# Decay attention in front of two MLPs: scores computed once, e normalised and transposed by TensorE, values' product in plain float32

## The chip, the cores and the metric

The kernel runs on one core of one Trainium2 chip. The metric is the device time of one execution in microseconds, the median of several runs. A profile of one execution gives, for each engine, every instruction with its start and its length. The engines are PE (TensorE), DVE (VectorE), ACT (ScalarE), POOL (GpSimd) and SP, whose queue issues most DMAs. The "granted clock" is the share of full speed at which TensorE was let run.

## The reference

Causal attention with a decay, over 4 batches of 8 heads with 576 positions of 64 numbers, feeds two MLPs over the 2304 tokens (512 to 2048 to 512 each).

```
scores = scale * np.matmul(q, k.transpose(0, 1, 3, 2))
cum    = np.cumsum(np.log(np.clip(f, 0.0001, 1.0)), axis=-1)
decay  = cum[:, :, :, None] - cum[:, :, None, :]
scores = np.where(causal, -1000000000.0, scores + decay)
scores = scores - np.max(scores, axis=-1, keepdims=True)
attn   = np.exp(scores)
attn   = attn / (np.sum(attn, axis=-1, keepdims=True) + 1e-09)
x      = np.matmul(attn, v)                       # heads side by side: 2304 x 512
h = x @ moe_w_in;  g = h * sigmoid(1.702 * h);  x2 = g @ moe_w_out
h = x2 @ moe2_w_in; g = max(h, 0) + alpha * min(h, 0); out = g @ moe2_w_out
```

## The kernel before

**Precision.** Where float32 accuracy is wanted, an operand is split into a rounded part in the type fp32r and the rest (hi and lo, by ACT L519 and by a subtraction, L524), and three fp32r products are added in PSUM: hi·hi, hi·lo, lo·hi. A plain float32 matmul does it in one instruction, more slowly.

**Units and chunks.** Attention goes by units of two heads of one batch, 16 in all, and a unit's queries in two chunks, 0 to 256 and 256 to 576 (CH). Batch 0, whose units come first chunk by chunk, uses the row-tiled path ("old" in the code): two heads at once, each in 64 rows of the array (L938, L1086), the operands transposed by TensorE (`load_pe`, L794). The other 12 units have stacked operands (`stack`; KA, KB, QA, QB), in which hi and lo parts and the rows for the decay share the 128 rows.

**What a chunk does.** `chunk` computes scores with queries in partitions, from the hi parts alone, to get each query's maximum: matmuls L925 to L938, a masked maximum by DVE (L952, with a second instruction that reads the accumulator), the two halves of the last 64 queries' row joined by POOL (L961). The maxima are turned into rows by TensorE (L969) and written, negated, into the query operand (L980 on ACT, L982 on DVE). `chunk2` then computes the scores again, all products, with keys in partitions (L1081, L1086); the subtraction of the maximum is part of the product. ACT takes the exponential (L1097, tile e); POOL zeroes the masked half of diagonal blocks (L998). `after_scores` splits e into eh (L519) and el (L524) and multiplies by the split values (L1044); narrow pieces and batch 0 use plain float32 instead (L1010 for the first chunk of batch 0, two heads each in 64 columns of the array; L1016). Columns of ones beside the values make the sums of e come out of the same matmuls. The result is normalised behind the product: in batch 0 and the last unit by transposes, a reciprocal and a multiplication on DVE (L1114 to L1130), elsewhere through copies u (L1136) and DMAs that spread the sums over partitions by way of a scratch in DRAM (`dscr`; L1139, L1144, L1146) with DVE's L1142, L1143 and L1150.

**Around it.** The normalised x lies in a ring `xr`. The first MLP's first product (L1180, 960 matmuls in blocks of 256, 320, 256, 320 and 384 tokens) runs as background work between the attention's matmuls. Behind attention come the rest of that product in another form (L1203), the second product (L1424), and the second MLP (L1203, L1606).

**What sets the order.** The class `Plan` collects all operations and schedules them once, when the program is built: by expected durations, priorities, tile pools and PSUM banks, a delay of 230 ns between engines (LAT), 105 ns for a change of tile mode on TensorE (SWITCH), and a holding-back of background work (TRIES). An operation may have several engines to choose from (`a_copy`, `a_out`, `a_sub`), where a bias by size (WC) holds DVE back for some. The result is a fixed program order on every engine, and every engine takes its own in order. Where the plan sees TensorE idle it puts in filler matmuls (L490). PSUM has eight banks, shared by pools with caps: ps_s (scores) 4, ps_m (maxima) 2, ps_v (value products) 3, ps_h (first MLP) 2, ps_x 2.

Of the kernel before, what the change touches and what calls it, by code (L numbers as in the profile page):

```python
# [16 lines left out]
BC = 0  # L17
WC = 1.2
# [7 lines left out]
SWITCH = 105.0  # L26
PADC = 8000.0
PAD0, PAD1, PADN, PADM = 1600.0, 130000.0, 220.0, 200.0
TRIES = [(60.0, 300.0, 400.0)]
# [56 lines left out]
class Plan:  # L86
# [37 lines left out]
    def plan(self, pen, hold_for, back):  # L124
# [27 lines left out]
        while avail:  # L152
# [95 lines left out]
def kernel(  # L248
# [51 lines left out]

    A0 = 100.0
# [12 lines left out]
    dscr = dram.tile([2 * BH, 2 * (S - SPLIT)], F32, name="dscr")  # L314
# [64 lines left out]
    p_v0 = sl("r", F32, [SPLIT // P, 2, P], (3, 0, NP))  # L379
    p_dq0 = sl("w", F32R, [1, SPLIT], (0, 8192, NP))  # L380
# [13 lines left out]
    p_z = sb("att", "Z", 2, [P, 2, P], F32R)  # L394
# [28 lines left out]
    ps_s = psum_pool(4)  # L423
    ps_m = psum_pool(2)
    ps_v = psum_pool(3)
# [61 lines left out]
    ident_r = const.tile([P, P], F32R, name="ident_r")  # L487
# [14 lines left out]
    b_id, b_idr, b_mask, b_mask2, b_cum, b_alpha = Buf(), Buf(), Buf(), Buf(), Buf(), Buf()  # L502
# [29 lines left out]
    def a_out(n):  # L532
        return [("ACT", c_act(n, True)), ("DVE", c_dve(n), BC + WC * n)]

# [42 lines left out]
    plan.add(a_copy(P), lambda e: copy(e, ident_r, ident), [b_id], [b_idr], -60)  # L577

    b_id2 = Buf()
    for i in range(2):  # L580
        plan.add(a_copy(64), lambda e, r=slice(64 * i, 64 * i + 64): copy(e, ident2[r], ident[r, r]), [b_id], [(b_id2, i)], -39)
    fill = {}

    def fills(rd, *sets):
        for nm, p, view, n, val, which in sets:
            for i in range(p.n)[which]:
# [4 lines left out]
                ], rd, [b], -40 if rd else -90 if nm == "mx" else -70)  # L591
# [1086 lines left out]
```

## Time and profile before

| | us |
|---|---|
| median of 3 runs | 978.47 (976.31 to 980.2) |
| the profiled execution, device time | 978.25 |
| its span in the profile | 976.5 |
| TensorE busy in the span | 958.9 (98%) |
| VectorE busy | 755.6 (77%) |
| ScalarE busy | 629.3 (64%) |
| GpSimd busy | 130.7 (13%) |

The span is what the profile covers, from the first instruction to the last; the device time holds 1.75 us more around it. Attention takes the first 342 us of the span, mixed with the first MLP's background work; up to 42 us batch 0 starts up. In the rows further down, "x48" counts instructions; in a timeline row a run of equal instructions on one line is one row, with the start of the first and the time to the end of the last. TensorE overlaps one instruction's end with the next one's start, so the time that an instruction takes from the engine is the distance from its start to the next start.

### The profile page before, as it was taken

Reading aid. Unit: us, or ns where it says so; the run is one execution under the profiler, and the core shown is the slowest. Engines: PE = TensorE matmul, PEld = TensorE weight load, DVE = VectorE, ACT = ScalarE, POOL = GpSimd, SP = SyncE. Lnnn points to the kernel's source line nnn. Section 1 sums busy time; section 2 is a strip of 40 time slices with the busy share of each in tenths; the row PEclk is TensorE's granted clock in tenths of the full one; section 3 lists DMA queues with packets and bytes.
Section 4 is the critical chain, followed back from the end, with each engine's and each line's share of the span. In section 5 each row is a group of like instructions: output and inputs, shape, how many; then the busy total and the mean of one; then the engine's idle time right before and its main releaser. Section 6 shows DMA issues by size and latency. Waiting matters only on the chain.

```text
span 976.5 us, 18451 instructions
## 1 busy us (share of the span) xinstructions
PE 958.9 (98%) x6343; PEld 899.6 (92%) x6343; DVE 755.6 (77%) x1635; ACT 629.3 (64%) x1310; POOL 130.7 (13%) x273
## 2 busy tenths in 40 slices
PE   8999999999999999999999999999999999999998
PEld 6788899899999999988888988999999999999998
DVE  4889977788877699946558785788668967887876
ACT  6778986888777558867667795575555743333332
POOL 4236643222222102100000000000000000000000
PEclk9999999999999999999999999999999999999999
DMA  7866634444443136757888685778738495543523
GB/s 140 183 196 182 161 88 119 95 98 93 110 106 75 54 104 226 214 176 256 285 324 277 219 254 188 245 267 297 281 114 308 163 381 197 155 148 109 152 76 99
DMA packets 190015, 176.16 MB, mean 180 GB/s; under 512 B 106480, under 2 KB 164736, under 8 KB 187616
## 3 DMA queue, kind: packets, MB, share of 16 engines
q1 hardware_dynamic: 189904, 174.96, 58.1%
q8 instruction: 50, 0.82, 0.4%
q14 instruction: 45, 0.37, 0.1%
q10 hardware_dynamic: 16, 0.01, 0.0%
HBM read 110.95 MB, written 63.90 MB: 179 GB/s over the span
## 4 chain that ended last, share of the span: by engine, by line
PE 82%; DVE 7%; ACT 4%; DMA 3%; issue 2%; SPq 1%; POOL 1%; DVEq 0%; ACTq 0%; POOLq 0%
PE bk L1203 23%; PE bk L1424 20%; PE bk L1606 19%; PE bk L1180 8%; PE bk L1081 3%; PE bk L1016 2%; PE bk L1044 2%; DVE bk L952 1%; DMA u<-dscr 1%; PE bk L1086 1%; DVE el L524 1%; ACT e L1097 1%; PE bk L927 1%; DMA wraw<-in_moe_w_in_dram 1%; DVE KB L524 1%
## 5 line engine op out<-in xcount | busy, mean ns | idle before, releaser
L1203 PE MATMUL bk<-x,wS 128*128 128x384 f32 x912 | 160.4, 335 | 0.3 <-DVE lx L1229 0.2
L1203 PEld LDWEIGHTS bk<-x,wS 128*128 128x128 f32 x912 | 158.1, 188 | 1.2 <-DVE lx L1229 0.5
L1180 PE MATMUL bk<-xh,w 128*128 128x320 f32 (+2 forms) x640 | 156.6, 309 | 0.0
L1424 PE MATMUL bk<-lh,w 128*128 128x512 f32 (+1 forms) x640 | 146.9, 369 | 0.0
L1424 PEld LDWEIGHTS bk<-lh,w 128*128 128x128 f32 x640 | 112.9, 189 | 19.8
L1180 PEld LDWEIGHTS bk<-xh,w 128*128 128x128 f32 x640 | 111.3, 189 | 2.0 <-issue 1.4
L1180 PE MATMUL bk<-xl,w 128*128 128x320 f32 (+2 forms) x320 | 97.3, 304 | 0.1
L952 DVE CUSTOM_DVE_ANT_0 bk<-bk,mask 128x288 f32<-128x288 f32 (+4 forms) x160 | 74.9, 497 | 19.9 <-PE bk L927 17.1
L524 DVE TENSOR_TENSOR ll<-lx,lh 128x512 fp32r<-128x512 f32 (+1 forms) x80 | 50.9, 637 | 49.2 <-PE bk L1424 34.4
L519 ACT CAST x<-x 128x768 fp32r<-128x768 f32 (+3 forms) x57 | 47.3, 858 | 61.6 <-PE bk L1606 47.5
L1424 PE MATMUL bk<-ll,w 128*128 128x512 f32 (+1 forms) x320 | 81.2, 368 | 0.0
L1097 ACT ACTIVATE e<-bk 128x320 f32<-128x320 f32 (+4 forms) x224 | 63.2, 363 | 19.3 <-PE bk L1081 8.3
L1606 PE MATMUL bk<-wS,x 128*128 128x256 f32 x567 | 70.5, 284 | 0.0
L1606 PEld LDWEIGHTS bk<-wS,x 128*128 128x128 f32 x567 | 69.1, 192 | 0.0
L524 DVE TENSOR_TENSOR x<-x,x 128x768 fp32r<-128x768 f32 (+3 forms) x59 | 57.0, 983 | 15.4 <-ACT x L519 15.0
L1606 PE MATMUL bk<-wS,lh 128*128 128x256 f32 x378 | 68.7, 284 | 0.0
L1424 PEld LDWEIGHTS bk<-ll,w 128*128 128x128 f32 x320 | 57.1, 189 | 9.7
L519 ACT CAST lh<-x 128x768 fp32r<-128x768 f32 (+3 forms) x38 | 31.4, 851 | 53.7 <-PE bk L1606 48.4
L1390 ACT ACTIVATE lx<-lx 128x512 f32<-128x512 f32 (+1 forms) x80 | 46.8, 587 | 29.6 <-DVE ll L524 27.0
L1180 PEld LDWEIGHTS bk<-xl,w 128*128 128x128 f32 x320 | 60.5, 189 | 0.8 <-DVE xl L524 0.3
L1606 PEld LDWEIGHTS bk<-wS,lh 128*128 128x128 f32 x378 | 59.0, 192 | 0.0
L519 ACT COPY lx<-bk 128x384 f32<-128x384 f32 x72 | 34.2, 479 | 33.2 <-PE bk L1203 18.0
(230 smaller groups left out, 2153.8 us busy)
## 6 DMA issues: line engine op xcount, KB each, us to landing
h2scr<-lx SPq DMA_DIRECT2D x96, 192.0 KB
wraw<-in_moe_w_in_dram SPq DMA_DIRECT2D x32, 512.0 KB
wraw<-in_moe_w_out_dram SPq DMA_DIRECT2D x32, 512.0 KB
lx<-h1scr SPq DMA_DIRECT2D x64, 256.0 KB
x<-h2scr SPq DMA_DIRECT2D x32, 512.0 KB
w2scr<-wS SPq DMA_DIRECT2D x5, 1792.0 KB
tscr<-wS SPq DMA_DIRECT2D x4, 1792.0 KB
wS<-tscr SPq DMA_DIRECT2D x4, 1792.0 KB
```

What stands on the lines that cost most here:

```text
L519: nc.scalar.copy(dst, src)
L524: E[e].tensor_tensor(dst, a, b, op=ALU.subtract)
L952: plan.add([("DVE", c_dve(c1 - c0))], lambda e, pm=pm, c0=c0, c1=c1, mk=mk, m0=m0, col=col, f0=f0: nc.vector.tensor_tensor_reduce(pm.ap[:, ...
L1016: nc.tensor.matmul(pb[hh].ap[:, c0:c1], vr.ap[:, t, hh, :], e32.ap[:, hh, e0:e0 + m], start=st, stop=sp, skip_group_check=True,)
L1044: nc.tensor.matmul(pb[hh].ap[:l.shape[1], s0 - q0:n], l, rhs.ap[:w, hh, :m], start=st, stop=sp, skip_group_check=True,)
L1081: nc.tensor.matmul(pss[hh].ap[:w, o_:o_ + m], x.ap[r, hh, a:a + w], y.ap[r, hh, s0 - q0:n], start=i == 0, stop=i == 1, skip_group_check=True)
L1097: plan.add([("ACT", c_act(x1 - x0, True))], lambda e, hh=hh, pss=pss, e32=e32, w=w, x0=x0, x1=x1: nc.scalar.activation(e32.ap[:w, hh, :x1 ...
L1180: nc.tensor.matmul(ph.ap[:, :n], w.ap[:, a, c, :], x[c // 2].ap[:, c % 2, :n], start=(c == 0 and j == 0), stop=(c == KT - 1 and j == 2))
L1203: nc.tensor.matmul(out.ap[:, :XH], wt(a, c), x.ap[:, b, c, :], start=(st and c == 0 and i == 0), stop=(c == 1 and i == 2), skip_group_chec ...
L1390: plan.add([("ACT", c_act(n))], lambda e: nc.scalar.activation(g.ap[:, :n], raw.ap[:, :n], AF.Gelu_apprx_sigmoid), [raw], [g], pri)
L1424: nc.tensor.matmul(py[d].ap[:, :n], w[:, a, d * P:(d + 1) * P], (lo if x else h).ap[:, :n], start=(k == 0 and (a, x) == (0, 0)), stop=(k = ...
L1606: nc.tensor.matmul(py[j].ap[:, t * HF:(t + 1) * HF], x.ap[:, q:q + P], w[:, o, a, :], start=(k == 0 and t == 0 and c == 0), stop=(k == NPA ...
```

## The change

Scores are computed once, with queries in partitions and all products (`chunk`: L915 row-tiled, L919 stacked, L908 for the last 64 queries through Z, which now holds hi and lo parts). DVE's masked reduction (L935) scales by −0.125 and takes the minimum, which stays as a column `ms` beside the queries. ACT's exponential (L944) uses that column as its bias and returns the row's sum into `ms`, over a tile ea, eb, ec or ed. DVE adds 1e-9 (L953; L949 adds the two halves of the last 64 queries too) and takes the reciprocal (L955), and e is scaled in place by it (`a_scale`: 84 times on POOL, L963, 60 times on ACT, L961). `chunk2` transposes e in blocks of 128×128 on TensorE (L994, 400 of them, plain float32), copies the blocks out of PSUM into eT (`a_out`, L512 on ACT 167 times, L514 on DVE 73 times), and multiplies values by eT in plain float32, two heads at once, each in 64 columns of the array (L1003). One copy takes the result to `xr`. The second pass of scores, the maxima's transposes and their negated copies, POOL's masks and L961, the splits of e and of the values, the copies u, the old normalisation and its 110 DMAs through `dscr` are gone. The identity in fp32r and the fills for ones columns are gone as well. Scores have 3 PSUM banks, transposes 3, value products 1; the tiles eb, ec, ed have one buffer each and eT three. The constants for the plan change too: WC from 1.2 to 0.6, a bias of its own for copies out of PSUM (WO_ = 0.3), 800 instead of 400 ns of holding back, 540 instead of 610 ns for issuing a DMA.

```
-WC = 1.2
+WC = 0.6
+WO_ = 0.3
-TRIES = [(60.0, 300.0, 400.0)]
+TRIES = [(60.0, 300.0, 800.0)]
-                free[QUEUE[eng]] = t + 610.0
+                free[QUEUE[eng]] = t + 540.0
...
-    ps_s = psum_pool(4)
-    ps_m = psum_pool(2)
-    ps_v = psum_pool(3)
+    ps_s = psum_pool(3)
+    ps_e = psum_pool(3)
+    ps_v = psum_pool(1)
...
     def a_out(n):
-        return [("ACT", c_act(n, True)), ("DVE", c_dve(n), BC + WC * n)]
+        return [("ACT", c_act(n, True)), ("DVE", c_dve(n), BC + WO_ * n)]
...
+    def a_scale(n):
+        return [("POOL", 280.0 + 0.8 * n, 0.0, True), ("ACT", c_act(n) + 30.0, 300.0), ("DVE", c_dve(n, True), 600.0, True)]
...
+                    for hh in range(2):
+                        for i, (x, y, r) in enumerate(((qb, kb, slice(0, P)), (qa, ka, slice(0, 66 if hh == 0 else P)))):
+                            nc.tensor.matmul(pms[hh].ap[:, f0:f0 + c1 - c0], x.ap[r, hh, a - q0:a - q0 + w], y.ap[r, hh, c0:c1], start=i == 0, stop=i == 1, skip_group_check=True)
...
-                        pm.ap[:, f0:f0 + c1 - c0], pm.ap[:, f0:f0 + c1 - c0], mk[:, m0:m0 + c1 - c0], 1.0, NEG,
-                        ALU.add, ALU.max, accum_out=mx.ap[:, col:col + 1],
+                        pm.ap[:, f0:f0 + c1 - c0], pm.ap[:, f0:f0 + c1 - c0], mk[:, m0:m0 + c1 - c0], -0.125, first(),
+                        ALU.add, ALU.min, accum_out=ms.ap[:, col:col + 1],
...
+                plan.add([("ACT", c_act(x1 - x0, True) + 30.0)], lambda e, pm=pm, t_=t_, i=i, x0=x0, x1=x1, f0=f0, mc=mc, sc=sc: nc.scalar.activation(
+                    view[t_, i](x0, x1), pm.ap[:, f0:f0 + x1 - x0], AF.Exp, scale=-1.0, bias=ms.ap[:, mc:mc + 1], accum_out=ms.ap[:, sc:sc + 1]
...
+                plan.add([("DVE", 70.0, 0.0, True)], lambda e, j=j: nc.vector.tensor_scalar_add(ms.ap[:, 6 + 2 * j:8 + 2 * j], ms.ap[:, 6 + 2 * j:8 + 2 * j], 1e-9), (), [(ms, ("s", 6 + 2 * j)), (ms, ("s", 7 + 2 * j))], pri)
...
+            plan.add([("DVE", 85.0)], lambda e, cs=cs: nc.vector.reciprocal(ms.ap[:, cs[0]:cs[-1] + 1], ms.ap[:, cs[0]:cs[-1] + 1]), (), [(ms, ("s", c)) for c in cs], pri)
...
+                        nc.tensor.transpose(pt.ap[:, i * P:(i + 1) * P], view[j, hh](t * P, t * P + P), ident)
...
+                for c0, c1, o in moves:
+                    plan.add(a_out(c1 - c0), lambda e, pt=pt, et=et, c0=c0, c1=c1, o=o: copy(e, et.ap[:, o:o + c1 - c0], pt.ap[:, c0:c1]), [pt], [(et, o)], pri)
...
+                    nc.tensor.matmul(
+                        pb.ap[64 * hh:64 * hh + 64, s0 - q0:n], vr.ap[:, t, hh], et.ap[:, hh * m:hh * m + m],
+                        start=t == 0, stop=t == nt - 1, skip_group_check=True, tile_position=(0, 64 * hh),
+                    )
...
+            plan.add(a_out(y - x), lambda e, x=x, y=y: copy(e, xr[:, hp, x % RING:x % RING + y - x], pb.ap[:, x - t0:y - t0]), [pb], keys, pri)
```

The plan is made anew, so the order changes on every engine. Three places:

On TensorE in the middle of attention, in the order before, the maxima's transposes, background matmuls and the second scores follow one another (bk is a PSUM bank, xh, xl and w are the first MLP's operands, MX the maxima):

```order
L969 MATMUL bk_92<-ident_r,MX_105 67x128 x2
L969 MATMUL bk_92<-ident_86,MX_105 67x64
L1180 MATMUL bk_89<-xh_1012,w_1036 128x256
L1180 MATMUL bk_89<-xl_650,w_1036 128x256
L1180 MATMUL bk_89<-xh_1012,w_1036 128x256 x2
L1180 MATMUL bk_89<-xl_650,w_1036 128x256
L1180 MATMUL bk_89<-xh_1012,w_1036 128x256
L927 MATMUL bk_88<-KA_409,QA_406 128x128
L927 MATMUL bk_87<-KA_409,QA_406 128x128
L1081 MATMUL bk_94<-QB_120,KB_117 64x64
```

and in the order after, transposes of e, background matmuls (there L1044) and the column-tiled value products of one chunk:

```order
L994 MATMUL bk_90<-ident,ec_556 128x128 x2
L994 MATMUL bk_90<-ident,ed_103 128x128
L994 MATMUL bk_86<-ident,ed_103 128x128
L1044 MATMUL bk_88<-xh_454,w_99 128x320
L1044 MATMUL bk_88<-xl_576,w_99 128x320
L1044 MATMUL bk_88<-xh_454,w_99 128x320 x2
L1044 MATMUL bk_88<-xl_576,w_99 128x320
L1044 MATMUL bk_88<-xh_454,w_99 128x320
L1003 MATMUL bk_87<-eT_352,VR_102 64x320 x2
L1003 MATMUL bk_87<-eT_398,VR_102 64x320 x2
L1003 MATMUL bk_87<-eT_346,VR_102 64x320 x2
L1003 MATMUL bk_87<-eT_352,VR_102 64x192 x2
```

Where two kinds of matmul of one tile shape stood, the shape changes once into the value products and once out of them. In all TensorE changes shape 39 times in attention before and 95 times after; fillers go from 30 to 43.

On DVE, a unit's maxima before, with the el split and the old normalisation (cd) between them (ISA is the masked reduction and, as 128x1, the read of its accumulator):

```order
L1142 TENSOR_SCALAR cd_475<-cd_475 128x5
L952 ISA bk_92,MX_105<-bk_92,mask 128x512
L952 ISA MX_105 128x1
L1143 RECIPROCAL cd_475<-cd_475 128x5
L524 TENSOR_TENSOR el_1427<-e_112,eh_1412 128x2x256
L735 STREAM_TRANSPOSE tk_595<-raw_142 128x320
L952 ISA bk_87,MX_105<-bk_87,mask 128x288
L952 ISA MX_105 128x1
```

and after, the minima with the add (L953) and the reciprocal (L955) of the same chunk's sums:

```order
L935 ISA bk_88,ms_278<-bk_88,mask 128x512
L935 ISA ms_278 128x1
L514 CAST Z_100<-QB_1126 128x64
L721 STREAM_TRANSPOSE tk_605<-raw_423 128x576
L953 TENSOR_SCALAR ms_278<-ms_278 128x2
L935 ISA bk_87,ms_278<-bk_87,mask_83,ms_278 128x288
L935 ISA ms_278 128x1
L514 COPY gg_742<-bk_86 128x320
L955 RECIPROCAL ms_278<-ms_278 128x2
L514 CAST KA_308<-tk_605 64x576
```

L953 needs the sums that ACT's exponentials return, and stands ahead of the next tile's minimum.

On TensorE at the end of attention, before, the last value products and what follows:

```order
L1044 MATMUL bk_92<-eh_1544,VL_116 128x320
L1044 MATMUL bk_87<-el_1572,VH_114 128x320
L1044 MATMUL bk_92<-el_1572,VH_114 128x320
L1180 MATMUL bk_90<-xh_1012,w_940 128x384
L1180 MATMUL bk_90<-xl_531,w_940 128x384
```

and after:

```order
L1003 MATMUL bk_89<-eT_352,VR_102 64x320 x2
L1003 MATMUL bk_89<-eT_398,VR_102 64x192 x2
L1003 MATMUL bk_89<-eT_346,VR_102 64x64 x2
L1044 MATMUL bk_86<-xh_567,w_1068 128x320
L1044 MATMUL bk_86<-xl_576,w_1068 128x320
```

Attention ends a whole block of the first MLP earlier: behind the last value product come 96 of the 960 background matmuls before, those of the 384-token block, and 282 after, beginning with the 320-token block.

## Rows read from the trace of the kernel before

**Rows 1.** Windows: length, busy (count) PE, PEld, DVE, ACT, POOL; clock; DMA share, GB/s

```profile
42.00:342.00 300.00, 290.84 (x2107) 272.84 (x2105) 242.02 (x645) 236.48 (x598) 104.10 (x209) 1.00 0.47 118
430.00:977.00 547.00, 542.03 (x3428) 513.23 (x3426) 408.37 (x747) 301.35 (x530) 0.00 (x0) 1.00 0.64 216
```

**Rows 2.** Timeline of TensorE in mid-stage: start, length, line, operands, rows*columns of array

```profile
236.04 0.27 PE L1081 MATMUL bk<-QB,KB 128*128 128x128 f32 x1
236.15 0.27 PE L1081 MATMUL bk<-QA,KA 128*128 128x128 f32 x1
236.46 0.56 PE L1044 MATMUL bk<-eh,VH 128*128 128x320 f32 x2
...
238.50 0.46 PE L1044 MATMUL bk<-el,VH 128*128 128x320 f32 x2
238.79 0.52 PE L927 MATMUL bk<-KA,QA 66*128 66x384 f32 x2
239.15 0.28 PE L1180 MATMUL bk<-xh,w 128*128 128x256 f32 x1
239.27 0.27 PE L1180 MATMUL bk<-xl,w 128*128 128x256 f32 x1
...
239.85 0.63 PE L927 MATMUL bk<-KA,QA 66*128 66x512 f32 x2
240.32 0.28 PE L1180 MATMUL bk<-xh,w 128*128 128x256 f32 x1
```

**Rows 3.** Groups, 0 to 342 us: xcount, busy, mean ns, idle before, what ended it

```profile
L952 DVE CUSTOM_DVE_ANT_0 bk<-bk,mask 128x288 f32<-128x288 f32 (+4 forms) x160 | 74.9, 497 | 19.9 <-PE bk L927 17.1 <-PE bk L938 1.8 <-PE bk L925 0.3
L524 DVE TENSOR_TENSOR el<-e,eh 128x640 fp32r<-128x640 f32 (+1 forms) x44 | 34.1, 788 | 4.9 <-ACT eh L519 4.7
L952 DVE DVE_READ_ACCUMULATOR2_ANT MX<- 128x1 fp32r x160 | 21.4, 134 | 0.4
...
L982 DVE TENSOR_SCALAR QA<-bk 3x256 fp32r<-3x256 f32 (+1 forms) x27 | 11.8, 438 | 14.8 <-ACT QA L980 10.0 <-PE bk L969 3.8 <-ACT eh L519 0.4
...
L1097 ACT ACTIVATE e<-bk 128x320 f32<-128x320 f32 (+4 forms) x224 | 63.2, 363 | 19.3 <-PE bk L1081 8.3 <-PE bk L1086 3.2 <-DVE cd L1120 2.4
L519 ACT CAST eh<-e 128x640 fp32r<-128x640 f32 (+1 forms) x47 | 32.5, 702 | 2.5 <-PE bk L1044 1.3 <-DVE cd L1142 0.5
...
L1136 ACT COPY u<-bk 128x256 f32<-128x256 f32 (+1 forms) x44 | 15.5, 405 | 6.5 <-PE bk L1044 3.6 <-PE bk L1016 2.8
```

**Rows 4.** The chain that ended last: start, length, what

```profile
129.94 4.35 DMA u<-dscr
```

**Rows 5.** Timeline of TensorE: plain float32 value products on the whole array

```profile
45.69 3.36 PE L1016 MATMUL bk<-e,VR 128*128 128x320 f32 x16
48.98 0.50 PE L938 MATMUL bk<-KA,QA 64*128 64x512 f32 x2
```

**Rows 6.** Timeline of TensorE: transposes, column-tiled value products, row-tiled scores

```profile
13.45 0.88 PE L794 MATMUL bk<-ident,r 128*128 128x128 f32 x6
14.16 0.83 PE L490 MATMUL bk<-ident 128*128 128x128 f32 x6
...
21.80 1.52 PE L1010 MATMUL bk<-e,r 128*64 128x256 f32 x16
23.25 0.74 PE L1086 MATMUL bk<-w,w 64*128 64x256 f32 x8
23.82 0.28 PE L938 MATMUL bk<-w,w 64*128 64x256 f32 x2
```

**Rows 7.** Timeline of TensorE: into row-tiled work and out of it

```profile
43.09 0.28 PE L1180 MATMUL bk<-xh,w 128*128 128x256 f32 x1
43.30 0.71 PE L1086 MATMUL bk<-QA,KA 64*128 64x320 f32 x6
...
44.09 0.39 PE L1180 MATMUL bk<-xh,w 128*128 128x256 f32 x1
44.31 0.28 PE L1180 MATMUL bk<-xl,w 128*128 128x256 f32 x1
```

More of the change, by code (lines that the diff above doesn't have):

```diff
@@ L849, in rows @@
                 ), [*((b_cum, (p_, i)) for p_ in range(len(ends)) for i in range(2)), *fdk], [(dk, (i, p_)) for p_ in range(len(ends)) for i in range(2)], pri)
-        if old and not pet:
-            split(load_qk(k, b, h0, n, 0, pri, actq), n, kh, kl, pri)
-            rows()
-        elif pet:
+        if old:
             for i, (lo, hi) in enumerate(ends):
@@ L942, in chunk @@
                 else:
-                    rd = [*([(qa, ("h", 0, 0)), (qa, ("h", 1, 0)), (qa, ("d", 0)), (qa, ("d", 1))] if w == P else [z]), *kn(c1)]
-                plan.add([("PE", 2 * c_mm(c1 - c0, P))], mm, rd, [(x, f0) for x in pms], pri, mode=1 if w == P and old else 0,
+                    rd = [*((x, (y, hh, p_)) for x, y in ((ka, "h"), (kb, "h"), (kb, "l")) for hh in range(2) for p_ in pr(c1)), (ka, ("d", 0)), (ka, ("d", 1))]
+                rd += [z] if w < P else [qh, ql] if old else [qa, qb]
@@ L945, in chunk @@
+                plan.add([("PE", 4 * c_mm(c1 - c0, P))], mm, rd, [(x, f0) for x in pms], pri, mode=1 if w == P and old else 0,
                     pad=(pms[0], lambda x=pms[0], f0=f0, n=min(P, c1 - c0): x.ap[:, f0:f0 + n], 4 if pri == A0 and j == 0 else 0))
                 for i, pm in enumerate(pms):
-                    col = 204 + (c0 > 0) if w < P else 68 * j + 64 * i if old else 68 * j + 66 * (1 - i)
+                    col = 4 + (c0 > 0) if w < P else 2 * j + i
                     if w == P:
@@ L1134, in chunk2 @@
-        rs, c, row = Buf(), n // 64, 2 * row + (q0 > 0)
-        for hh in range(2):
-            plan.add([("ACT", c_act(n, True))], lambda e, hh=hh: nc.scalar.copy(u_.ap[:, hh, :n], pb[hh].ap[:, :n]), [pb[hh]], [(u_, hh)], pri)
-        for hh in range(2):
-            r = 64 - 64 * hh
-            plan.add(DMA(4 * n), lambda e, hh=hh, r=r: nc.sync.dma_start(
-                cd.ap[64 * hh:64 * hh + 64, :c], u_.ap[r:r + 1, hh, :n].rearrange("o (p c) -> o p c", c=c)
-            ), [(u_, hh)], [(cd, hh)], pri)
@@ L1142, in chunk2 @@
-        plan.add([("DVE", 75.0, 0.0, True)], lambda e: nc.vector.tensor_scalar_add(cd.ap[:, :c], cd.ap[:, :c], 1e-9), (), [cd], pri)
-        plan.add([("DVE", 100.0)], lambda e: nc.vector.reciprocal(cd.ap[:, :c], cd.ap[:, :c]), (), [cd], pri)
-        plan.add(DMA(8 * n), lambda e: nc.sync.dma_start(dscr[row, :2 * n].rearrange("(q c) -> q c", c=c), cd.ap[:, :c]), [cd], [rs], pri)
-        for hh in range(2):
-            plan.add(DMA(256 * n), lambda e, hh=hh: nc.sync.dma_start(
-                u_.ap[64 * hh:64 * hh + 64, 1 - hh, :n], dscr[row, hh * n:hh * n + n].partition_broadcast(64)
-            ), [rs], [(u_, 1 - hh)], pri)
```

420 lines of the change are left out of this document (148 added, 272 removed).

## The prediction

> **What bounds the kernel now.** I read the windows by stage first, because shares of the whole span mix two kinds of work. From 430 us to the end TensorE is busy 542.03 of 547.00 us, the other engines much less, at a granted clock of 1.00 [rows 1]. The change touches nothing there, so this stretch keeps its length. The attention stage is the row 42 to 342: TensorE busy 290.84 of 300.00, VectorE 242.02 (share .81), ScalarE 236.48 (.79), GpSimd 104.10 [rows 1]. TensorE is the bound here too, but with two close followers. "Busy" hides something, because a matmul that waits can still be drawn as the long tail of the one before it. So I read the timeline by start-to-start steps. Full-array fp32r matmuls step .11 us for 128 columns (236.04 to 236.15), .12 for 256 (239.15 to 239.27), .145 for 320 (two between 238.50 and 238.79), .18 for 384 and .235 for 512 [rows 2]. But from 236.15 to 236.46 a 128-column matmul takes .31 instead of .11: the next one waits for `eh`, and the .20 us is a hold-up, not work [rows 2]. Priced by these steps, the work in the stage comes to about 282 of its 300 us, my estimate from these steps and the instruction counts, so some 18 us are hold-ups. The group rows name their sources: VectorE idles 19.9 us before L952, 4.9 before `el`, 14.8 before L982, ScalarE 19.3 before the exponentials [rows 3]; the chain of waits goes once through the sums' DMA round trip for 4.35 us [rows 4].
>
> **The change on TensorE.** TensorE is the bound, so the sum is made there, a "unit" being two heads of one batch: 12 units on the stacked path (batches 1 to 3), 4 on the row-tiled path (batch 0).
>
> Stacked unit before: maxima scores 2×(.11+.12+.18+.235)+4×.135 = 1.83 (.135 for 288 columns, between 256 and 320); the maxima's transposes .3 (five matmuls, at half to all of .11); second scores 4×(.11+.12)+12×.145+4×.11+4×.06 = 3.34 (the last for 64 columns, half of 128); value products 6×.12+18×.145 = 3.33 in split form and 768 columns in plain float32 at 3.29 us for 1792 columns, 1.84 ns each (16 matmuls, 45.69 to 48.98 [rows 5]), 1.41. Together 10.2.
>
> After: scores once but with all products, 4×(.11+.12+.18+.235)+8×.135 = 3.66. Then 25 transposes of 128×128 plain float32. The trace has such transposes at L794, six from 13.45 to 14.16, .118 each [rows 6]; in longer runs I take the .11 of a 128-column matmul, 2.75 a unit. Then 1600 columns of value products with two heads side by side in 64 columns of the array each. L1010 is that form: 16 matmuls, 768 pairs of columns, from 21.80 to 23.25, 1.89 ns a pair [rows 6], so 3.02. Together 9.43: .78 us less, times 12 = 9.4.
>
> Batch-0 unit before: row-tiled pairs step .071 a 256-column matmul (eight from 23.25 to 23.82 [rows 6]), .28 ns a column. First scores 2.0 (four matmuls over 1280 columns, and 4×.135 for the last 64 queries), maxima's transposes .3, second scores (eight matmuls over 1600 columns) 3.6, value products 1.45 (L1010) and 4.47 (2432 columns at 1.84 ns): 11.8. After: 2.85 + 1.08 + 2.75 + 3.02 = 9.7. That is 2.1 less, times 4 = 8.4. Work saved: 18 us.
>
> Against it stand **changes of tile shape**. Row-tiled work between full-array work costs .09 on entering (43.09 to 43.30, .21 for .12) and .10 on the first matmul after it (44.09 to 44.31, .22) [rows 7]. By the instruction order TensorE changes shape 95 times instead of 39. The 1.89 ns already holds about half of the 56 more; 28 at .09 to .19 are 2.5 to 5.3, I take 4. The Trainium skill (TensorEngine Tiling (Array Packing), Key Properties) says that a change of tiling mode drains TensorE; [rows 7] agree, and without that the sum would be 4 us lower. The order also holds 13 more filler matmuls, .11 each if they delay anything: 0 to 1.4, I take 1. **Net 13 us**: 978.25 − 13 = 965.
>
> **The other engines**, which this holds only if they keep up. ScalarE loses in the stage e (63.2), `eh` (32.5) and `u` (15.5): 111 [rows 3]. By busy time per instruction (63.2/224 = .28 at 229 columns on average, 15.5/44 = .35 at 288) it gains 160 exponentials of 314 columns on average at .37 (59), 167 of the 240 copies of transposed e at .28 (47), 24 result copies (8) and 60 scalings of e at about .40 (24): 138. Net +27, less the negated maxima and the values' split, without rows here, which bring it towards 0. The trace shows no exponential that also returns its row sum: between nothing and .134 each (what VectorE's read of an accumulator takes, L952's second row [rows 3]) that is 0 to 21. I take the low end and keep the other for the range. VectorE loses `el` (34.1), L982 (11.8) and the old normalisation; it gains 80 small adds, 80 reciprocals and 73 copies of transposed e. At .13 for a small one (the accumulator read) and .35 a copy that is 21 + 26 = 47: about even or some us less. GpSimd gets 84 scalings and loses the diagonal masks, L961 and most fills; half idle today (104.10 of 300.00), it has room, but e waits for it before the transposes.
>
> The stage also becomes **denser**. In the order before, 96 of 960 first-MLP matmuls stand behind the last value product, in the order after 282. At .15 us those 186 (28 us) leave the attention stage and come after it, where they cost the same. The stage shrinks from 300 to about 259, with nearly the same ScalarE work less 31 copies of first-MLP results (11 us): ScalarE's share goes from .79 to between .87 (226/259) and 1.05 (236.5+27−11+21 = 273), VectorE's from .81 to about .9.
>
> SP loses 110 DMAs (the sums' way through `dscr`), so everything queued there moves up; that removes the 4.35 us wait of [rows 4]. I count nothing for it: L1150 behind it is off TensorE's path unless the first MLP waits for it. PSUM: scores get 3 banks instead of 4, transposes 3, value products 1 instead of 3; so a unit's value products end before the next one's begin, behind one copy (.35 us, 32 times), covered by the first-MLP matmuls placed between.
>
> **Forecast and rivals.**
> F, the forecast: work saved shows, hold-ups stay about 18 us. 965; with the shape changes at either end, and the hold-ups half as many or half as many more (±9), 955 to 973. Chance .41.
>
> A, hold-ups vanish: split chain, L982 and the DMA round trip go, and transposes are fed by copies that run well ahead. Up to 18 more: 947. For it: VectorE's 14.8 us before L982 and 4.9 before `el` have no successor of the same kind. Against it: new chains are as long (minimum, exponential, add, reciprocal, scaling, transpose, copy, product). Chance .14.
>
> B, ScalarE paces the stage. At 273 us of work in 259 the stage is 14 us longer, and the 13 saved are given back: 979, no change. For it: the upper sum above. Against it: fillers in the order rise only to 43, and durations on ScalarE overlap. Chance .21.
>
> C, slower: VectorE's new small add stands in its in-order queue behind ScalarE's sums, and the next tile's minimum, on which a PSUM bank and hence TensorE's next scores wait, stands behind the add. The order shows it: two heads' minima, two or three short instructions, the add, the next minimum. Its price is that of the nearest wait of VectorE for a chain over other engines: 14.8/27 = .55 us before L982 [rows 3]. 80 of them are 44 us, less the 14.8 that go: +29, 994. It decides from .41 us a wait (33 us over 80), where the sum reaches 983. Against it: where ScalarE runs ahead the add waits for nothing. Chance .21.
>
> T, TensorE's clock falls during transposes. The windows show a granted clock of 1.00, that is 2.4 GHz [rows 1], and L794's transposes run at the pace of matmuls [rows 6]. If 400 transposes ran at 1.2 GHz they would take 47 us more (400×.118): 1012. The Trainium skill (TensorE: Matmul & The Clock Gate, Part 4: PE-mode transpose) states that transposes do not count as busy time for the clock and gives 275 ns for one; the trace's .118 us speaks against it. Chance .03.
>
> **How the numbers follow.** The likeliest is F, 965. F, B and A lie between 947 and 979; with the bounds on shape changes, row sums and ScalarE's share, and leaving out most of C and T, the range is 943 to 990. About 0.5% (973.4 to 983.4) is what a measurement of this kernel can tell from no change. F without its slowest end and A: faster .54; B and a bit of F: .22; C, T and B's upper end: .24.
>
> **What would show it.** The start steps of L994 should be .11, of L1003 pairs 1.9 ns a column, the granted clock 1.00. The last value product should come some 40 us earlier than today, followed by about 186 more first-MLP matmuls; if it comes earlier by less than 28 us, the change is no gain. For A, no step in mid-stage above its form's own. For B, ScalarE busy over 95% of the stage and TensorE waiting for copies into eT. For C, VectorE idle before L953, released by ScalarE, of over .4 us each, and TensorE's scores late after it. Wrong altogether would be a changed length of the stretch behind the first MLP.

## The result and the profile after

The changed kernel takes 988.8 us (988.2 to 989.4, 4 runs) against 979.3 of before in the same runs: 1.0099 times the time before, 95% interval 1.007 to 1.0128. It is about 1% slower, where 965 and a gain of 13 us had been forecast. The profiled execution took 989.04 us, its span is 987.2.

The windows of the changed kernel, with the columns of [rows 1] (length; busy time of PE, PEld, DVE, ACT, POOL; granted clock):

```profile
42.00:342.00 300.00, 274.81 (x2002) 231.46 (x2002) 243.11 (x743) 255.41 (x745) 145.76 (x135) 0.99 0.41 101
430.00:987.00 557.00, 551.84 (x3468) 520.57 (x3466) 427.89 (x793) 278.44 (x500) 0.00 (x0) 1.00 0.64 215
```

In this window of 300 us TensorE's busy time falls from 290.84 to 274.81, so it stands idle for 25 us instead of 9: it waits. ScalarE's busy time rises from 236.48 to 255.41 and GpSimd's from 104.10 to 145.76. Behind attention TensorE is as full as before.

The timeline of TensorE round the last value product, first two rows of before, then two of the changed kernel:

```profile
342.03 0.46 PE L1044 MATMUL bk<-el,VH 128*128 128x320 f32 x2
342.33 0.34 PE L1180 MATMUL bk<-xh,w 128*128 128x384 f32 x1
...
319.03 2.39 PE L1003 MATMUL bk<-eT,VR 128*64 128x320 f32 x20
321.34 0.41 PE L1044 MATMUL bk<-xh,w 128*128 128x320 f32 x1
```

The first-MLP matmul behind the last value product starts at 321.34 instead of 342.33, so attention ends 21 us earlier. The prediction wanted some 41, and had set 28 us as the point under which the change is no gain, since the 186 first-MLP matmuls that are pushed behind attention take 28 us or more there. What is behind it follows from the waits. The view of what TensorE waited for in 0 to 342 us (total, times, longest), the longest row of before and then three of the changed kernel:

```profile
PE bk L1044 <- ACT eh L519: 3.7, 4, 1.9
...
PE bk L994 <- POOL ed L963: 7.8, 5, 2.2
PE bk L994 <- ACT eT L512: 4.2, 6, 1.0
PE bk L994 <- POOL ec L963: 3.7, 3, 2.3
```

The transposes of e wait for GpSimd to scale e. The groups of these scalings by shape (count | busy, mean ns | idle before):

```profile
L963 POOL TENSOR_SCALAR ec<-ec,ms 128x512 f32<-128x512 f32 x20 | 32.9, 1650 | 31.0 <-DVE ms L955 22.2 <-ACT ed L944 4.6 <-ACT KA L512 4.2
L963 POOL TENSOR_SCALAR ea<-ea,ms 128x256 f32<-128x256 f32 x21 | 20.2, 971 | 9.5 <-DVE ms L955 6.5 <-ACT ea L944 1.7 <-ACT ea L961 0.9
L963 POOL TENSOR_SCALAR eb<-eb,ms 128x384 f32<-128x384 f32 x15 | 19.2, 1277 | 55.0 <-DVE ms L955 45.8 <-PE bk L919 4.6 <-ACT eT L512 2.5
L963 POOL TENSOR_SCALAR ed<-ed,ms 128x576 f32<-128x576 f32 x10 | 18.4, 1841 | 5.4 <-DVE ms L955 3.3 <-ACT ec L944 2.0
L963 POOL TENSOR_SCALAR ea<-ea,ms 128x128 f32<-128x128 f32 x18 | 11.0, 615 | 27.7 <-DVE ms L955 17.2 <-ACT eT L512 9.2 <-ACT ea L944 1.2
```

The plan reckons with 280 ns + 0.8 ns a column, 690 ns for 512 columns; the chip takes 1650. In all that is 102 us of GpSimd where the plan put 47, and each scaling lies on the chain from a chunk's scores to its value product. Two more things that the plan and the prediction did not have are in ScalarE's groups. The first two rows are of before, the others of the changed kernel:

```profile
L1097 ACT ACTIVATE e<-bk 128x256 f32<-128x256 f32 x32 | 12.5, 397 | 6.8 <-PE bk L1086 2.8 <-DVE cd L1120 2.4 <-issue 1.2
L1097 ACT ACTIVATE e<-bk 128x128 f32<-128x128 f32 x32 | 7.1, 282 | 0.4 <-PE bk L1010 0.4
...
L944 ACT ACTIVATE ea<-bk,ms 128x256 f32<-128x256 f32 x32 | 15.1, 480 | 0.2 <-DVE ms L955 0.2
L944 ACT ACTIVATION_READ_ACCUMULATOR ea<-bk,ms 128x1 f32 x64 | 13.3, 208 | 0.0
L944 ACT ACTIVATE ea<-bk,ms 128x128 f32<-128x128 f32 x32 | 11.7, 371 | 2.6 <-DVE ms L935 2.4
```

An exponential with its bias in a column takes 83 to 89 ns more than one without, and the sum of a row needs a second instruction. How much of ScalarE that second one takes stands in its timeline, changed kernel:

```profile
176.18 0.37 ACT L944 ACTIVATE ea<-bk,ms 128x128 f32<-128x128 f32 x1
176.44 0.20 ACT L944 ACTIVATION_READ_ACCUMULATOR ea<-bk,ms 128x1 f32 x1
176.53 0.47 ACT L944 ACTIVATE ea<-bk,ms 128x256 f32<-128x256 f32 x1
176.89 0.20 ACT L944 ACTIVATION_READ_ACCUMULATOR ea<-bk,ms 128x1 f32 x1
176.98 0.42 ACT L512 COPY gg<-bk 128x320 f32<-128x320 f32 x1
```

From the start of a read to the next start it is .09 us. Over 160 exponentials, bias (.09) and sum (.09) are about 29 us of ScalarE, an estimate from these rows.

### The profile page after: what moved, and what is told of

It is laid out like the page before. It is cut to its first block, busy times and chain, and to the rows that moved or that the text cites. A ratio compares the mean times of both kernels' runs of the same rounds, so it can differ in the third digit from the quotient of the medians.

```text
span 987.2 us, 18126 instructions
## 1 busy us (share of the span) xinstructions
PE 951.6 (96%) x6225; PEld 864.8 (88%) x6225; DVE 753.2 (76%) x1752; ACT 621.8 (63%) x1446; POOL 174.7 (18%) x180
## 4 chain that ended last, share of the span: by engine, by line
PE 70%; ACT 6%; DVE 6%; DMA 3%; issue 1%; POOL 1%; SPq 0%; DVEq 0%; ACTq 0%; POOLq 0%
PE bk L1288 20%; PE bk L1067 19%; PE bk L1470 18%; PE bk L1044 7%; PE bk L1003 2%; PE bk L994 2%; DMA h2scr<-lx 2%; DVE bk L935 1%; PE bk L919 1%; ACT ea L944 1%; ACT eT L512 1%; ACT ed L944 1%; POOL ed L963 1%; DVE ms L953 0%; DMA raw<-in_q_dram 0%
## 5 line engine op out<-in xcount | busy, mean ns | idle before, releaser
L1044 PE MATMUL bk<-xh,w 128*128 128x320 f32 (+2 forms) x640 | 147.0, 306 | 3.6 <-DVE w L517 2.9
L1044 PEld LDWEIGHTS bk<-xh,w 128*128 128x128 f32 x640 | 109.1, 189 | 6.6 <-DVE w L517 3.5
L1044 PE MATMUL bk<-xl,w 128*128 128x320 f32 (+2 forms) x320 | 97.2, 304 | 0.2 <-DVE xl L517 0.2
L517 DVE TENSOR_TENSOR ll<-lx,lh 128x512 fp32r<-128x512 f32 (+1 forms) x80 | 50.8, 635 | 48.9 <-PE bk L1288 37.1
L512 ACT CAST x<-x 128x768 fp32r<-128x768 f32 (+3 forms) x41 | 33.4, 825 | 67.5 <-PE bk L1470 55.2
L935 DVE CUSTOM_DVE_ANT_0 bk<-bk,mask 128x128 f32<-128x128 f32 (+4 forms) x144 | 68.5, 495 | 8.8 <-ACT ea L944 4.1
L512 ACT CAST lh<-x 128x768 fp32r<-128x768 f32 (+3 forms) x29 | 23.2, 805 | 63.3 <-PE bk L1470 48.6
L1044 PEld LDWEIGHTS bk<-xl,w 128*128 128x128 f32 x320 | 60.4, 189 | 0.8 <-DVE xl L517 0.7
L512 ACT COPY lx<-bk 128x384 f32<-128x384 f32 x72 | 34.2, 479 | 38.8 <-PE bk L1067 25.1
L517 DVE TENSOR_TENSOR x<-x,x 128x768 fp32r<-128x768 f32 (+3 forms) x59 | 55.9, 979 | 3.4 <-ACT x L512 2.4
L512 ACT COPY eT<-bk 128x256 f32<-128x256 f32 (+5 forms) x167 | 49.4, 357 | 14.3 <-PE bk L994 6.1
```

Of the source, the lines that this page charges most:

```text
L512: nc.scalar.copy(dst, src)
L517: E[e].tensor_tensor(dst, a, b, op=ALU.subtract)
L935: plan.add([("DVE", c_dve(c1 - c0) + 50.0)], lambda e, pm=pm, c0=c0, c1=c1, mk=mk, m0=m0, col=col, f0=f0, first=first: nc.vector.tensor_te ...
L1044: nc.tensor.matmul(ph.ap[:, :n], w.ap[:, a, c, :], x[c // 2].ap[:, c % 2, :n], start=(c == 0 and j == 0), stop=(c == KT - 1 and j == 2))
```

## The experiments

**What the new costs are worth in the changed kernel's own order.** Four runs keep every engine's order and leave out one cost or more; the times compare with 988.8 (the kernel before took 979.1 to 980.1 beside all the runs below).

GpSimd's scalings cut to 64 columns:

```
-                        E[e].tensor_scalar_mul(x, x, ms.ap[:, c:c + 1])
+                        E[e].tensor_scalar_mul(x[:, :64], x[:, :64], ms.ap[:, c:c + 1])
```

> The changed kernel with one edit: GpSimd's 84 scalings of e (L963) take only the first 64 columns of their piece, so the rest of those pieces stays unscaled. The program order of every engine is the same. In the changed kernel's trace these scalings take 0.62 us for 128 columns up to 1.84 us for 576, about 108 us of GpSimd in all, and TensorE waits for ec, ed and ea of them. If GpSimd's slow scaling is the main cause of the missing 24 us (theory P), this runs 10 to 18 us faster than the changed kernel's 988.8, at 971 to 979, and the two dips of TensorE's granted clock go. If ScalarE's reads of the row sums are the main cause (theory S), it gains under 5 us: 984 to 989. If neither, but the order itself (one buffer each for eb, ec and ed, one PSUM bank for value products) is, under 5 us too.

Measured: 979.8, 9.1 us faster. The wait for ed falls from 7.8 us to .3, in the same view of this run:

```profile
PE bk L994 <- ACT eT L512: 4.9, 10, 0.9
PE bk L1003 <- ACT eT L512: 3.3, 6, 1.4
PE bk L1003 <- DVE eT L514: 0.9, 2, 0.5
PE bk L994 <- DVE eT L514: 0.6, 1, 0.6
PE bk L994 <- POOL ed L963: 0.3, 1, 0.3
```

That is a little less than theory P wanted and more than the others allow: GpSimd is the largest cause, not the only one. The two dips of the granted clock in the stage are gone, as expected, but this run's profile has another one in the start-up, where the changed kernel's has none. The window of the changed kernel, then of this run:

```profile
0.00:42.00 42.00, 37.03 (x260) 26.02 (x261) 26.29 (x113) 33.71 (x101) 17.15 (x33) 1.00 0.77 160
0.00:42.00 42.00, 37.76 (x241) 26.94 (x241) 23.49 (x101) 31.38 (x93) 11.02 (x31) 0.88 0.75 155
```

By the mean of .88 that is up to 5 us that this run does not get back. What brings it is not shown, so 9.1 us is the gain of the whole kernel and not a clean price of the scalings.

VectorE's add no longer waits for the sums (the reciprocal and the scalings read the new columns 18 to 22, so they too can come before the sums):

```
-nc.vector.tensor_scalar_add(ms.ap[:, 6 + 2 * j:8 + 2 * j], ms.ap[:, 6 + 2 * j:8 + 2 * j], 1e-9)
+nc.vector.tensor_scalar_add(ms.ap[:, 18 + 2 * j:20 + 2 * j], ms.ap[:, 2 * j:2 * j + 2], 1e-9)
```

> The changed kernel with one edit: VectorE's small add (L953, L949), and with it the reciprocal and the scaling, reads the minima instead of the row sums, so e is scaled by a wrong number; the exponentials still return their sums, which nobody uses. Orders are the same on all engines. This takes away VectorE's wait for ScalarE's sums, the mechanism of rival C, and nothing else. VectorE's idle time before L953 is 15.8 us for 64 adds, 0.25 us each. If C were the cause (the in-order add delays the next minimum), up to 15 us come back: 974 to 980. If the waits at the add lie beside other waits (theories P and S), 0 to 5 us: 984 to 989.

Measured: 984.9, 3.9 us faster. VectorE's group row for the add, in the changed kernel and then in this run:

```profile
L953 DVE TENSOR_SCALAR ms<-ms 128x2 f32<-128x2 f32 x64 | 16.4, 260 | 15.8 <-ACT ea L944 6.9 <-ACT eb L944 6.9 <-ACT ec L944 1.4
...
L953 DVE TENSOR_SCALAR ms<-ms 128x2 f32<-128x2 f32 x64 | 14.2, 228 | 0.4
```

Nearly all of the 15.8 us of idle time goes, and the kernel gets 3.9 us. Rival C's mechanism exists, at no more than about an eighth of its price of 29 us; the shorter chain to the scalings is part of the 3.9.

The same, and no sums at all:

```
-..., bias=ms.ap[:, mc:mc + 1], accum_out=ms.ap[:, sc:sc + 1]
+..., bias=ms.ap[:, mc:mc + 1]
```

> As the one before, and the exponentials return no row sums: 160 reads of an accumulator by ScalarE fall away, each 93 ns from start to the next start, and the exponentials step about 90 ns shorter as well (250 ns for 128 columns with a sum, against 160 in the kernel before). That is about 29 us less ScalarE work in the attention stage. Theory S, that these reads are the main cause: 970 to 977. Theory P: 0 to 6 us beyond the run without the wait at the add, 980 to 989.

Measured: 980.2, 4.7 us beyond the run before, so 15 us of reads cost 4.7. One part of the expectation was wrong: the exponentials themselves did not get shorter. A 128-column one still steps .27 us in this run's timeline:

```profile
174.64 0.37 ACT L944 ACTIVATE ea<-bk,ms 128x128 f32<-128x128 f32 x1
174.91 0.42 ACT L512 COPY gg<-bk 128x320 f32<-128x320 f32 x1
```

So it is not the sum that makes them longer. What is left of the difference between this exponential and that of before is the bias column (and another constant as scale); no run took that out.

The first and the third together:

> The edits of the first and the third run together: GpSimd's scalings cut to 64 columns, no row sums, the add reading the minima. If GpSimd and the sums together are what was missing from the forecast, the time is the forecast's, 960 to 968. If both lie on the same chains and do not add up, 968 to 975. If the order itself holds TensorE up, over 975.

Measured: 968.9, 19.9 us faster than the changed kernel and 10 faster than before. Apart, the cuts had given 9.1 and 8.6 us. Its end of attention and its window from 42 to 300 us:

```profile
298.24 2.07 PE L1003 MATMUL bk<-eT,VR 128*64 128x320 f32 x18
300.23 0.41 PE L1044 MATMUL bk<-xh,w 128*128 128x320 f32 x1
```

```profile
42.00:300.00 258.00, 246.70 (x1853) 207.10 (x1853) 208.54 (x712) 228.08 (x583) 86.50 (x133) 1.00 0.45 111
```

Attention ends at 300, where the prediction's 41 us less (342 to 301) puts it. As a whole the sum for TensorE came out; what was missing is what GpSimd and ScalarE do to it. Its terms are not separated by this run.

**By which way GpSimd costs.** After each cut scaling of more than 144 columns GpSimd does about the rest of its old work on a scratch tile, `scr`:

```
-                        E[e].tensor_scalar_mul(x, x, ms.ap[:, c:c + 1])
+                        (E[e].tensor_scalar_mul(x[:, :64], x[:, :64], ms.ap[:, c:c + 1]), ext > 144 and E[e].tensor_scalar_mul(scr[:, :ext - 144], scr[:, :ext - 144], ms.ap[:, c:c + 1]))
```

> The changed kernel as in the run with GpSimd's scalings cut to 64 columns (979.8), but after each cut scaling GpSimd multiplies as many columns of a scratch tile as were cut (less 80 for the second instruction's start), so GpSimd works as long as in the changed kernel, while e is ready early. Orders are unchanged. If what the long scalings cost is e coming late to the transposes, this stays near 980 (978 to 982). If it is mostly that VectorE's short instructions wait until a running GpSimd instruction ends, the time goes back towards 988.8 (985 to 989).

Measured: 981.0. GpSimd, as busy in the stage as in the changed kernel (148.90 us, against 145.76), costs 1.2 us when e is handed on early, against 9.1 when e waits for it. So it is e's lateness.

**The constants of the plan.**

The kernel before with the constants after, and the reverse; the first edit is

```
-WC = 1.2
+WC = 0.6
+WO_ = 0.3
...
-TRIES = [(60.0, 300.0, 400.0)]
+TRIES = [(60.0, 300.0, 800.0)]
...
-                free[QUEUE[eng]] = t + 610.0
+                free[QUEUE[eng]] = t + 540.0
...
-        return [("ACT", c_act(n, True)), ("DVE", c_dve(n), BC + WC * n)]
+        return [("ACT", c_act(n, True)), ("DVE", c_dve(n), BC + WO_ * n)]
```

> The kernel before, with the changed constants of the plan and nothing else (WC 0.6, copies out of PSUM with a bias of 0.3, 800 ns of holding back, 540 ns for issuing a DMA). The prediction counted nothing for the constants. If they are worth nothing by themselves, 975 to 984. If they carry part of the loss, over 984; if they help the old kernel too, under 975.

> The changed kernel planned with the constants of before (WC and the bias of copies out of PSUM 1.2, 400 ns, 610 ns). ScalarE then gets more of the copies and casts, VectorE fewer. If ScalarE is as full as its unexpected reads of row sums make it, this is 3 to 12 slower than the changed kernel, 992 to 1001. If the constants do not matter, 985 to 992.

Measured: 988.0 for the kernel before with the new constants, 989.2 for the changed kernel with the old ones. They cost the old kernel 9 us and change nothing in the new one, so taking them back wins nothing of this loss. Whether they cost something once the plan has true durations (below) was not run. ScalarE had 272.29 us in the stage with the old constants instead of 255.41, and it made no difference.

**The same work, planned with its true durations.** The changed kernel with three numbers corrected in the plan, the last the exponential's (the second run has only the first, GpSimd's):

```
-        return [("POOL", 280.0 + 0.8 * n, 0.0, True), ("ACT", c_act(n) + 30.0, 300.0), ...
+        return [("POOL", 230.0 + 2.85 * n, 0.0, True), ("ACT", c_act(n) + 100.0, 300.0), ...
...
-                plan.add([("ACT", c_act(x1 - x0, True) + 30.0)], ...
+                plan.add([("ACT", c_act(x1 - x0, True) + 190.0)], ...
```

> The changed kernel, nothing left out, planned with the durations that its trace shows: a scaling of e on GpSimd at 230 ns + 2.85 ns a column (instead of 280 + 0.8), on ScalarE 70 ns dearer, an exponential with its row sum 160 ns dearer. The plan then gives GpSimd 21 of the 144 scalings instead of 84, ScalarE 68 and VectorE 55; 240 of the first MLP's matmuls stand behind the last value product instead of 282. If what was wrong with the changed kernel is that its order was made for scalings and exponentials shorter than they are, 966 to 974. If the dearer work itself is too much for three engines, whatever the order, VectorE and ScalarE set the pace: 978 to 986.

> As the run with all true durations, but only that of GpSimd's scalings is corrected; exponentials and ScalarE's scalings are planned as in the changed kernel. The plan gives GpSimd 25 scalings, ScalarE 75, VectorE 44. In the runs of the first call GpSimd's scalings were worth 9 us and the sums 9 (half of it the wait at the add). If the plan's wrong duration for GpSimd alone made half of the damage, 974 to 982, that is 4 to 10 slower than with all true durations. If ScalarE gets fuller and its sums weigh more for it, 983 or more.

Measured: 978.6 with all three, and 986.8 with GpSimd's number alone. The first gets back 10 us and ends where the kernel before is (ratio 0.9997, 0.9987 to 1.0006), which is the second branch of its expectation: the dearer work is too much. The other falls into the branch of 983 or more: with GpSimd relieved the plan loads ScalarE (75 scalings instead of 60) while it still reckons the exponentials too short, and ScalarE has 260.26 us in 42 to 342. With all three numbers VectorE has 267.65 us there, ScalarE 249.76:

```profile
42.00:342.00 300.00, 285.10 (x2063) 242.21 (x2062) 267.65 (x831) 249.76 (x729) 64.09 (x77) 0.99 0.42 105
```

Is what remains the work, or this order? Three runs cut it in the order made from true durations: all 144 scalings to 64 columns, the sums (by the edits of the third run), and both. Of the scalings now ScalarE's are cut too:

```
-                        nc.scalar.mul(x, x, ms.ap[:, c:c + 1])
+                        nc.scalar.mul(x[:, :64], x[:, :64], ms.ap[:, c:c + 1])
```

> The kernel with all true durations (978.6), its orders unchanged, with all 144 scalings of e, on GpSimd, ScalarE and VectorE, cut to the first 64 columns. If what keeps that kernel 10 us above the changed order without these costs (968.9) is the work itself, this is 4 to 8 faster, 970 to 975. If the order made from true durations is worse by itself, 976 to 980.

> The kernel with all true durations, its orders unchanged, with exponentials that return no row sums and with the add reading the minima; the scalings are whole, by a wrong number. If the reads of the sums cost as much here as in the changed order (4.7, and 3.9 for the wait), 970 to 975. If they are hidden once the order reckons with them, 976 to 980.

> Both cuts together in the order made from true durations. If the work is what costs, 965 to 971, like the changed order with both cuts (968.9). If the order is worse by itself, 972 or more.

Measured: 971.0, 975.5 and 967.6. Without both, either order gives 968 (967.6, and 968.9 where of the scalings only GpSimd's were cut). The scalings cost 7.7 and the sums 3.1 us even when the plan knows them (9.0 and 3.8 by the ratios to the kernel before, which was 1 us slower beside these runs). So of the 19.9 us about 10 come back with an order made for true durations, and what remains is the work.

**Versions meant to beat both.** VectorE preferred for the scalings, two buffers for eb, ec and ed, no adds of 1e-9:

```
-    EB, ET = 1, 3
+    EB, ET = 2, 3
...
-        return [..., ("ACT", c_act(n) + 100.0, 300.0), ("DVE", c_dve(n, True), 600.0, True)]
+        return [..., ("ACT", c_act(n) + 100.0, 600.0), ("DVE", c_dve(n, True), 300.0, True)]
```

> As the run with all true durations, with VectorE preferred for the scalings (123 of 144), two buffers each for eb, ec and ed instead of one, without the 64 adds of 1e-9 (the sums are at least 1, where 1e-9 does not change a float32), and the best of nine settings for holding background work back instead of one. If VectorE has the room (its share in the changed kernel's attention stage is 0.82) the time is 958 to 966, under both kernels. If VectorE becomes the bound, its shares in the stage go over 0.95 and the time is 968 to 980.

Measured: 980.3, just above the 968 to 980 that the expectation gave for VectorE as the bound. But VectorE is busy for 234.70 of the 258 us between 42 and 300 (.91), under the .95 that it named, so that VectorE is the bound is not shown; what holds TensorE there was not taken apart.

No scaling of e; the result is multiplied on its way out by the reciprocals, which TensorE turns into rows:

```
-                plan.add(a_scale(ext), sc_, [(ms, ("s", c))], ks, pri)
...
+                nc.tensor.transpose(pr.ap[:, j * P:(j + 1) * P], xx["rx"].ap[:, j], ident)
...
+            plan.add(a_out(w2), lambda e: copy(e, rs.ap[:, :w2], pr.ap[:, :w2]), [pr], [(rs, 0)], pri + RPRI)
...
+                xr[:, hp, x % RING:x % RING + y - x], pb.ap[:, x - t0:y - t0], rs.ap[:, x - t0:y - t0], op=ALU.mult), [pb, rs], keys, pri)
```

> The changed kernel without any scaling of e: e goes into the transposes as it is. VectorE writes the reciprocals of the sums repeated over 128 columns, 80 more transposes on TensorE turn them into rows, one copy per chunk takes these out of PSUM, and VectorE multiplies the result by them on its way to xr, in place of the plain copy. Planned with the exponential's true duration, without the adds of 1e-9 as in the tuned run. GpSimd gets no scaling, ScalarE loses 60 scalings, TensorE gains 80 transposes at .11 (9 us), and the sums are no longer on the chain from the exponential to the transpose. If the length of that chain is what holds the kernel with all true durations at 978.6, this runs at 962 to 972 in spite of TensorE's 9 us. If ScalarE's and VectorE's amount of work is the bound, whatever the chain, 975 to 985.

Measured: 1009.7, for a reason of its own. VectorE's row for the reciprocals written over 128 columns:

```profile
L959 DVE RECIPROCAL rx<-ms 128x128 f32<-128x128 f32 x80 | 74.8, 941 | 4.7 <-ACT eb L948 3.0 <-ACT ea L948 1.3
```

A reciprocal of two columns took 154 ns; 128 take 941, where the plan had put 210. With that mended, by a copy that repeats a reciprocal of two columns (in the second run not on GpSimd):

```
+            plan.add([("DVE", c_dve(P), 100.0, True), ("ACT", c_act(P) + 30.0, 200.0), ("POOL", 600.0, PB, True)], lambda e, cs=cs, j=j: copy(
+                e, rx.ap[:, j].rearrange("p (h o) -> p h o", h=len(cs)),
```

> As the run with late normalisation, but VectorE's reciprocal is small again (two columns) and a copy repeats it over 128 columns, 67 times on GpSimd and 13 times on ScalarE; best of nine settings for holding background work back. In the run before, the reciprocals over 128 columns took .94 us each, 75 us of VectorE, which was its error. If late normalisation as such is good, 965 to 974. If GpSimd, also for these small copies, holds VectorE up by the port they share or makes the chain to xr long, 975 to 985.

> As the run beside it, with the copies that repeat the reciprocals on VectorE (55) and ScalarE (25) instead of GpSimd and ScalarE: 10 us more work for VectorE, 4 for ScalarE, 40 less for GpSimd. If GpSimd's part is what costs, 963 to 972 and under the run beside it; if VectorE's and ScalarE's amount of work sets the pace, 3 to 8 us over the run beside it.

Measured: 977.7 (ratio 0.9991, 0.9974 to 1.0009) and 979.1. The scaling has gone from the chain, and with what took its place (80 copies, 80 transposes, the multiplications on VectorE) the time is that of the order made from true durations; which of them costs it was not taken apart. No version beat the kernel before by more than the measurement can tell.

## Why the prediction was wrong

- **The range.** 988.8 lies inside 943 to 990, but that is luck: the upper end stood there for rivals B and C, and the largest single cause, the wait for GpSimd's scalings, had no price in any of them.
- **TensorE's work: right as a whole.** L994 steps .11 us, as taken (91.80 to 91.91 below). The value products of 1216 column pairs run from 198.62 to 200.91, 1.88 ns a pair, for 1.89:

```profile
198.62 2.36 PE L1003 MATMUL bk<-eT,VR 128*64 128x320 f32 x20
200.91 0.33 PE L994 MATMUL bk<-ident,ea 128*128 128x128 f32 x1
```

  With the new costs cut out attention ends at 300, for 301, and the kernel takes 968.9, inside the forecast's own range of 955 to 973.
- **GpSimd's scalings: the step that failed.** The prediction gave them one sentence, "half idle today (104.10 of 300.00), it has room, but e waits for it before the transposes", and no price. By its own number GpSimd was a third busy, but room was the wrong question: 84 scalings of .6 to 1.8 us stand in the chain of their chunks, and TensorE waits behind it. [rows 3] had no row of GpSimd; the trace of before had some, as that of GpSimd's subtractions for the values' split in 42 to 342 us:

```profile
L524 POOL TENSOR_TENSOR VL<-VR,VH 128x384 fp32r<-128x384 f32 x7 | 7.3, 1049 | 14.0 <-ACT VH L519 7.4 <-DMA cd<-u 3.8 <-DMA raw<-in_q_dram 2.8
```

  That is 2.7 ns a column. Over the 29440 columns of the 84 scalings it makes about 80 us of GpSimd, an estimate from another kind of instruction; 102 were measured, and the plan put 47. What their lateness cost is 9.1 us by the run that cuts them, and 7.7 for all scalings in the order made from true durations.
- **The exponential with its sum: mis-sized.** It was taken at the low end, 0, with .134 each (21 us) as the high end. It is .09 for the read, and .09 more for the bias column, which the prediction did not price at all: 29 us of ScalarE, over the high end. The time it cost is 4.7 us for the reads. What the bias costs in time was not taken out in any run. ScalarE's 60 scalings were too small as well, .58 us of busy time each for .40, which is 11 us; the copies of transposed e were right, .30 for .28. Still ScalarE's whole work from 42 us to the end of attention, 244 us, lies between the prediction's 226 and 273; its sum is not what went out of range.
- **Rival C: seen, and mis-sized.** .25 us of idle time an add instead of .55, and 3.9 us at the end instead of 29. That the rest of the waits lies beside waits of others fits this, but was not shown one by one.
- **Rival B** came true in part: ScalarE's share of the 300 us is .85 (255.41 of 300), up from .79 but under B's sign of .95, and its reads of sums are part of the loss; GpSimd's lateness is the larger part. **Rival A** is out: in the changed kernel new waits (11.5 us for GpSimd alone) took the place of the old ones.
- **The stage behind attention** kept its pace: from the last value product to the end 31.7 us more (987.2 − 321.3 less 976.5 − 342.3) for 186 more matmuls, 90 of them of 320 columns (.147) and 96 of 384 (.174), which makes 30.
- Of the 24 us between 965 and 988.8 the runs show 19.9. The last 4, between 965 and 968.9, are within the forecast's own range and are not taken apart here.

**Rival T and the clock.** The granted clock did fall, twice, to .57 in these windows of the changed kernel:

```profile
92.00:96.00 4.00, 4.00 (x21) 3.04 (x21) 3.08 (x8) 2.61 (x8) 3.26 (x3) 0.57 0.65 131
232.00:236.00 4.00, 4.00 (x22) 2.71 (x22) 3.17 (x9) 2.82 (x9) 1.41 (x2) 0.57 0.04 6
```

The timeline of TensorE ahead of the first one tells what it did before (the last row is ahead of the second):

```profile
88.88 0.27 PE L994 MATMUL bk<-ident,eb 128*128 128x128 f32 x1
91.41 0.33 PE L994 MATMUL bk<-ident,ec 128*128 128x128 f32 x1 [2.26 <-POOL ec L963]
...
91.80 0.27 PE L994 MATMUL bk<-ident,ec 128*128 128x128 f32 x1
91.91 0.27 PE L994 MATMUL bk<-ident,eb 128*128 128x128 f32 x1
...
92.64 0.42 PE L994 MATMUL bk<-ident,eb 128*128 128x128 f32 x1
92.85 0.42 PE L994 MATMUL bk<-ident,ec 128*128 128x128 f32 x1
...
231.18 0.33 PE L994 MATMUL bk<-ident,ed 128*128 128x128 f32 x1 [1.57 <-POOL ed L963]
```

Ahead of the first it stood idle for 2.26 us waiting for a scaling, went on at .11 a transpose, and from about 92.3 on took .21: 1.2 instead of 2.4 GHz. The two stretches are 8 us at .57, so at most 3.4 us lost, and they are part of what GpSimd's lateness costs: in the run with cut scalings the stage has 1.00. Both falls come behind idle time, 2.26 and 1.57 us of waiting for a scaling. Transposes alone do not bring one: in the run with both cuts the same 400 transposes run in the same order, and the clock is 1.00 from 42 to 300 us. The Trainium skill (TensorE: Matmul & The Clock Gate, Part 4: PE-mode transpose) says that transposes do not count as busy in the same way; that run has no fall that would show it, but with other matmuls all around them no run here settles how they count. The prediction's argument with 275 ns for one compared a length with a step: the rows of L994 are .27 long too, and step .11.

## What to carry to other kernels

When a change puts a new engine into a chain, price its instruction from that engine's own rows, not by how idle the engine is; an engine with time to spare that is slow per column still makes everything behind it late. A plan that orders instructions by expected durations is only as good as these: three corrected numbers were worth 10 us here, more than the constants beside them. And when an order with a cost left out gives the forecast's time, the forecast's sum holds as a whole, and what it forgot is that cost.

## What the runs showed of the hardware

A VectorE instruction of two columns can wait for GpSimd. Here is one add of the changed kernel, and what GpSimd was doing:

```profile
177.11 1.99 POOL L517 TENSOR_TENSOR KB<-tk,KA 64x576 fp32r<-64x576 f32 x1
```

```profile
177.90 1.23 DVE L953 TENSOR_SCALAR ms<-ms 128x2 f32<-128x2 f32 x1
```

GpSimd's instruction ends at 179.10, the add at 179.13. Of the 80 adds (L953, L949), 33 start while a GpSimd instruction runs and take .44 us on average, the other 47 .16 (counted from the trace). The Trainium skill (SBUF — State Buffer, Who interferes with whom) says that the two engines share a pair of ports, and that where both use it the one that issues first holds it for its whole instruction; the rows agree. The run with GpSimd kept busy on a scratch tile prices what the long scalings do to VectorE in this way, together with that tile's own instructions, at 1.2 us here; GpSimd's subtractions (L517), as in the row above, are in both runs.

ScalarE's exponential took .08 to .09 us more with its bias in a column, and .09 for handing out a row's sum. VectorE's reciprocal took 941 ns for 128 columns, against 286 for a copy of as many out of PSUM.
